# A fused attention and gated feed-forward kernel: batch 0 loaded by hardware queues in fp32, GpSimd's loads gated, a new order on eight PSUM banks

## The chip, the cores and the metric

The kernel runs on one core of a Trainium2 chip. The metric is device time in microseconds (us) of one execution. It is longer than the span of the profile (first to last instruction).

A ratio in this document is the mean time of one kernel's fast runs over that of the other's fast runs of the same rounds. So it is not quite the ratio of the medians that are quoted beside it. "Before" ran beside everything: its median was 224.40 us in the first rounds and 225.06, 224.94, 224.89 and 225.20 us in the later ones. For that reason results of different rounds are compared by their ratios to before.

## The reference

```python
B, H, S, Ns, D = 8, 8, 512, 32, 64            # x: (B,H,S,D), state: (B,H,Ns,D), fp32
scores = x @ state^T / sqrt(D);  a  = softmax(scores);   xread = a  @ state     # 512 rows
scores2 = state @ x^T / sqrt(D); a2 = softmax(scores2);  sread = a2 @ x         #  32 rows
rows = concat([xread, sread])                 # per batch 544 rows of H*D = 512
out  = (relu(rows @ w_gate) * (rows @ w_val)) @ w_out      # d_ff = 1536, fp32 out
```

## The kernel before

The kernel folds the attention's second product into the feed-forward part. Per batch it makes U = state times a weight column block ("c" and "u" units). It then multiplies U by the transposed attention weights ("gv": four matmuls of 512 columns), applies relu on ScalarE and the product on VectorE, and multiplies by w_out ("o"). It has two parts. The first, for batches 0, 1 and some of 2, is an explicit list of steps; here it is called the ordered part. Its matmuls write into eight PSUM buffers, called banks, which are handed from step to step. The rest is a loop that the change doesn't touch.

```python
def x_T(b, j):                    # transposes of one pair of heads
    ...
    for c in range(NC):
        if b == 0 and j < 2:      # heads 0-3 of batch 0: cast on chip, 128x128 transposes
            nc.tensor.transpose(ps[:, c], x_head(b)[:, c, 2*j:2*j+2]..., id128)
        else:                     # cast on load: head-major layout, two 64-wide transposes
            for h2 in range(2):
                nc.tensor.transpose(ps[64*h2:64*h2+64, c], v[:, c, h + h2], id128)
...
def bank(name, kind="r"):         # the ordered part names its PSUM bank ("@3");
    if given: n = given.pop(0)    # the loop behind takes 0,1,2,... in turn
    ...
    else: n = turn["r"] % 6 if kind == "r" else 6 + turn["o"] % 2
...
for eng, j in ((nc.sync, 0), (nc.scalar, None), (nc.scalar, 1)):   # fp32, hardware queues
    ...                           # None: state of batches 0 and 1
make_identity(nc, id128)
...
xb_alloc(0)                       # heads 4-7 of batch 0, cast to bf16 by GpSimd's DMA
nc.gpsimd.dma_start(out=x_tail(0)..., in_=x[0, HK:H]...)
...
program = """                     # dx: batch load, dw: weight columns, xc: cast, spin: warm-up
dx.1.0.2 dx.1.1.2 stc.0.0.act stc.0.1.dve spin.7 stT.0@0 xc.0.0.dve dw.0.0.128 sto.0.act dw.1.0.128 on xc.0.1.dve
spin.3 xT.0.1@1 dw.0.128.128 xT.0.0@2 ... sc.0.0@3 ... xT.0.2@4 xT.0.3@5 ... sc.0.1@0 ...
... gv.2.0@21 mu.1.8 re.2.0 o.0.7 mu.2.0 o.0.8 o.0.9@7 of.0.2.dve sr.1@3 sn.1 xp.2 xp.3
"""
```

The softmax here doesn't subtract the row's maximum and nothing guards it: scores larger than these inputs give would overflow.

Of the kernel before, what the change touches and what calls it, by code (L numbers as in the profile page):

```python
# [16 lines left out]
def kernel(  # L17
# [37 lines left out]
    NK = 2  # L55
# [18 lines left out]
    tiny = const.tile([128, 1], FP32, name="tiny")  # L74

# [68 lines left out]
    def x_conv_pair(b, j, eng):  # L144
        dst = x_head(b)[:, :, 2 * j:2 * j + 2].rearrange("p c h d -> p h c d")
        copy[eng](out=dst, in_=xf[b][:, 2 * j:2 * j + 2])

    def x_head(b):
        return xb[b][:, 0:NC * HK * D].rearrange("p (c h d) -> p c h d", c=NC, h=HK)

    def x_tail(b):
        return xb[b][:, NC * HK * D:].rearrange("p (h c d) -> p c h d", c=NC, h=HK)
# [9 lines left out]
    def x_T(b, j):  # L162

        if b not in xT:
            xT_alloc(b)
        ps = bank("xT_ps").bitcast(BF16)[:, 0:512].rearrange("p (c t) -> p c t", c=NC)
        for c in range(NC):
            if b == 0 and j < 2:
                nc.tensor.transpose(ps[:, c], x_head(b)[:, c, 2 * j:2 * j + 2].rearrange("p h d -> p (h d)"), id128)
            else:  # L170
                v, h = (x_tail(b), 2 * j - HK) if b == 0 else (xb[b], 2 * j)
                for h2 in range(2):
                    nc.tensor.transpose(ps[64 * h2:64 * h2 + 64, c], v[:, c, h + h2], id128)
        held["xT", b, j] = ps
# [63 lines left out]
    def att_T2(b):  # L238
        ans_alloc(b)
        ps = held["aT2", b] = bank("aT_ps").bitcast(BF16).rearrange("p (k c t) -> p k c t", k=NK, c=NC)  # L240
        for kc in range(NK):
            for c in range(NC):
                nc.tensor.transpose(ps[:, kc, c], a_sn[b][:, kc, c], id128)

    def att_out2(b, eng):
        copy[eng](out=ANS[b], in_=held["aT2", b])

# [3 lines left out]
    def x_pad(b):  # L251

        v = xa[:, b % NX].rearrange("p (c h) d -> p h c d", c=NC)[:, :, :, 0:D]
        for hs, src in (((0, x_head(b)), (HK, x_tail(b))) if b == 0 else ((0, xb[b]),)):
            src = src.rearrange("p c h d -> p h c d")
            nc.gpsimd.tensor_copy(out=v[:, hs:hs + src.shape[1]], in_=src)  # L256
# [153 lines left out]

    xb_alloc(0)
    nc.gpsimd.dma_start(out=x_tail(0).rearrange("p c h d -> p h c d"),  # L412
                        in_=x[0, HK:H].rearrange("h (p c) d -> p h c d", c=NC))

    def x_load(b, part, parts):
        if part == 0:
            xb_alloc(b)
            xb[b] = xb[b].rearrange("p (h c d) -> p c h d", h=H, c=NC)
# [11 lines left out]
    def spin(n, cols=512):  # L430
        for i in range(n):
# [4 lines left out]
    steps = {"spin": spin, "stc": state_conv, "stT": state_T, "sto": state_out, "xc": x_conv_pair, "xT": x_T, "xT2": x_T2, "xo2": x_out2, "on": lambda: nc.gpsimd.memset(xa[:, :, :, D:D + 1], 1.0), "dw": w_load, "dx": x_load, "ds": lambda: state_dma(nc.gpsimd, 2, B), "do": wo_dma,  # L436
             "df": lambda b: x_dma(b, (nc.gpsimd,)), "xo": x_out,
             "sc": att_sc, "ex": att_exp, "nr": att_sum, "nx": att_scale, "aT2": att_T2, "ao2": att_out2, "aT": att_T, "ao": att_out,
# [3 lines left out]
    dx.1.0.2 dx.1.1.2 stc.0.0.act stc.0.1.dve spin.7 stT.0@0 xc.0.0.dve dw.0.0.128 sto.0.act dw.1.0.128 on xc.0.1.dve  # L442
    spin.3 xT.0.1@1 dw.0.128.128 xT.0.0@2 xo.0.1.dve xo.0.0.act dw.1.128.128 spin.3 sc.0.0@3 dw.0.256.256 ex.0.0
    spin.1 xT.0.2@4 xT.0.3@5 xo.0.2.dve dw.1.256.256 xo.0.3.act nr.0.0 spin.3 sc.0.1@0 dw.0.512.256 xT2.1.0@1 ex.0.1
    nx.0.0 xo2.1.0.act nr.0.1 dw.1.512.256 spin.2 xT2.1.1@2 xo2.1.1.act sc.1.0@3 dw.0.768.256 nx.0.1 ex.1.0
    dw.1.768.256 spin.2 c.1.0.128@45 c.0.0.128@01 co.1.0.128.0.dve aT.0.1@2 co.0.0.128.0.act aT.0.0@3 co.1.0.128.1.dve
    co.0.0.128.1.act dw.0.1024.256 sc.1.1@4 ao.0.1.dve ao.0.0.act nr.1.0 ex.1.1 dw.1.1024.256 spin.2 c.0.128.128@05
    gv.0.0@12 co.0.128.128.1.act nr.1.1 co.0.128.128.0.act nx.1.0.pool re.0.0 gv.0.1@34 mu.0.0 re.0.1 nx.1.1.pool
    c.1.128.128@50 mu.0.1 co.1.128.128.1.act c.0.256.256@12 co.1.128.128.0.act c.1.256.256@30 dw.0.1280.256
    co.0.256.256.0.dve co.0.256.256.1.act aT.1.1@5 aT.1.0@4 co.1.256.256.0.act co.1.256.256.1.dve dw.1.1280.256  # L450
    gv.0.3@21 ao.1.1.act ao.1.0.dve dx.2.0.1 re.0.3 gv.0.2@30 mu.0.3 ds re.0.2 c.1.512.256@54 mu.0.2 gv.1.2@21
    co.1.512.256.1.act co.1.512.256.0.act do.0.6 c.0.512.256@30 re.1.2 gv.1.5@45 co.0.512.256.0.dve xp.1
    co.0.512.256.1.act mu.1.2 re.1.5 gv.1.3@23 mu.1.5 re.1.3 gv.1.1@04 do.6.12 mu.1.3 re.1.1 c.1.768.256@15 xp.0
# [124 lines left out]
```

## Time and profile before

| before, first trace | |
|---|---|
| time | 224.46 us median of 3 runs (224.29 to 224.59) |
| span of the profiled execution | 223.9 us (its own time was 225.65 us) |
| TensorE busy | 96% |
| first weights of 128 columns landed | 11.6 and 12.3 us |
| first weight matmul, first gv | 12.38, 14.43 us |
| ordered part ends on TensorE | 57.28 us |

From the page of before come the span, the busy time of each engine with its share of the span, the DMA engines' busy share in 40 slices of 5.6 us (9 is 90% or more), and the chain of waits:

```profile
span 223.9 us, 4840 instructions
PE 215.5 (96%) x1937; PEld 105.8 (47%) x1967; DVE 129.0 (58%) x226; ACT 124.8 (56%) x236; POOL 53.0 (24%) x58
...
DMA  7999999070146671781159114511311111111132
...
PE 84%; DMA 9%; POOL 4%; issue 2%; DVE 0%; POOLq 0%; DVEq 0%
```

TensorE is the bottleneck, and the DMA engines are full from the second slice to the seventh (5.6 to 39 us). So only the start can move much: once data and weights are there, the matmuls are dense. Next the timeline of before (start, duration, engine, line, instruction). POOL is GpSimd; its DMA lines are the time in which it issues the load, not the transfer.

```profile
1.42 0.98 POOL L412 DMA_DIRECT2D xb<-in_x_dram  x1
2.40 1.50 POOL L420 DMA_DIRECT2D xb<-in_x_dram  x2
...
12.38 0.25 PE L291 MATMUL upc<-wg_sb,stT 64*32 64x128 bf16 x8
...
14.43 1.93 PE L316 MATMUL gv_ps<-ans,U 128*128 128x512 bf16 x8
```

GpSimd issues from 1.42 us on; the first weight matmul follows the landing of its weights (12.3) at once. The same start in windows of 1 us: for each engine its busy time, then the TensorE clock, the DMA share (1 or more means that the 16 engines are full) and the GB/s written:

```profile
4.00:5.00 1.00, 1.00 (x6) 0.56 (x6) 0.82 (x3) 0.30 (x2) 1.00 (x2) 1.00 1.30 241
5.00:6.00 1.00, 0.92 (x9) 0.42 (x8) 0.63 (x1) 0.56 (x1) 1.00 (x3) 1.00 1.28 165
6.00:7.00 1.00, 0.97 (x10) 0.36 (x8) 0.43 (x1) 0.58 (x1) 1.00 (x3) 1.00 1.35 179
```

The DMA share (last column but one) never falls below 1. A casting load reads twice what it writes, so 180 GB/s written is about 360 read.

### The profile page before, as it was taken

Reading aid. Unit: us, or ns where it says so; the run is one execution under the profiler, and the core shown is the slowest. Engines: PE = TensorE matmul, PEld = TensorE weight load, DVE = VectorE, ACT = ScalarE, POOL = GpSimd, SP = SyncE. Lnnn points to the kernel's source line nnn. Section 1 sums busy time; section 2 is a strip of 40 time slices with the busy share of each in tenths; the row PEclk is TensorE's granted clock in tenths of the full one; section 3 lists DMA queues with packets and bytes.
Section 4 is the critical chain, followed back from the end, with each engine's and each line's share of the span. In section 5 each row is a group of like instructions: output and inputs, shape, how many; then the busy total and the mean of one; then the engine's idle time right before and its main releaser. Section 6 shows DMA issues by size and latency. Waiting matters only on the chain.

```text
span 223.9 us, 4840 instructions
## 1 busy us (share of the span) xinstructions
PE 215.5 (96%) x1937; PEld 105.8 (47%) x1967; DVE 129.0 (58%) x226; ACT 124.8 (56%) x236; POOL 53.0 (24%) x58
## 2 busy tenths in 40 slices
PE   7899999999999999999999999999999999999994
PEld 2544354444544444444444444444444445666543
DVE  3587888757595648663876468646874433222100
ACT  4599877865467644665557456545655444222221
POOL 8698828503302434006000700000000000000000
PEclk9999999999999999999999999999999999999999
DMA  7999999070146671781159114511311111111132
GB/s 157 176 195 197 215 225 278 24 187 3 47 106 225 112 267 47 160 265 50 50 118 276 49 60 99 107 50 47 94 50 47 48 47 50 48 64 74 54 94 94
DMA packets 37799, 25.48 MB, mean 114 GB/s; under 512 B 18864, under 2 KB 33200, under 8 KB 37776
## 3 DMA queue, kind: packets, MB, share of 16 engines
q1 hardware_dynamic: 24912, 16.85, 26.2%
q0 software_dynamic: 11968, 7.47, 21.5%
q10 hardware_dynamic: 896, 0.85, 1.4%
q8 instruction: 15, 0.25, 0.4%
q14 instruction: 8, 0.07, 0.1%
HBM read 18.35 MB, written 8.91 MB: 122 GB/s over the span
## 4 chain that ended last, share of the span: by engine, by line
PE 84%; DMA 9%; POOL 4%; issue 2%; DVE 0%; POOLq 0%; DVEq 0%
PE o_ps L353 38%; PE gv_ps L316 31%; DMA xb<-in_x_dram 9%; PE gv_ps L333 5%; PE up L291 4%; PE sr_ps L264 1%; POOL wv_sb L110 1%; PE sc_ps L200 1%; PE o_ps L379 1%; POOL wg_sb L110 1%; POOL a_sn L219 1%; PE xT_ps L186 0%; POOL xb L412 0%; PE stT_ps L129 0%; POOL xb L420 0%
## 5 line engine op out<-in xcount | busy, mean ns | idle before, releaser
L316 PE MATMUL gv_ps<-ans,U 128*128 128x512 bf16 x373 | 93.9, 380 | 0.5
L353 PE MATMUL o_ps<-wo_sb,h_sb 128*128 128x512 bf16 x357 | 91.6, 380 | 2.1 <-issue 1.9
L344 DVE TENSOR_TENSOR h_sb<-gv_ps,g_sb 128x512 bf16<-128x512 f32 x96 | 65.3, 689 | 44.2 <-ACT g_sb L340 43.3
L340 ACT ACTIVATE g_sb<-gv_ps 128x512 bf16<-128x512 f32 (+1 forms) x108 | 62.7, 580 | 49.3 <-PE gv_ps L316 34.5
L316 PEld LDWEIGHTS <-U 128*128 128x128 bf16 x384 | 35.8, 98 | 40.5 <-issue 0.6
L353 PEld LDWEIGHTS <-h_sb 128*128 128x128 bf16 x372 | 35.2, 98 | 39.9 <-issue 1.7
L361 ACT COPY o_sb<-o_ps 128x512 f32<-128x512 f32 x29 | 17.1, 590 | 16.5 <-PE o_ps L353 16.5
L301 ACT CAST U<-up 128x512 bf16<-128x512 f32 x36 | 18.9, 594 | 11.4 <-PE up L291 11.4
L301 DVE CAST U<-up 128x512 bf16<-128x512 f32 x36 | 22.8, 684 | 2.2 <-PE up L291 1.9
L142 POOL CAST xb<-xf 128x1024 bf16<-128x1024 f32 x10 | 10.1, 1040 | 53.6 <-DMA xf<-in_x_dram 32.6
L256 POOL COPY xa<-xb 128x2048 bf16<-128x2048 bf16 (+1 forms) x9 | 15.7, 1747 | 11.5 <-issue 6.6
L213 DVE TENSOR_REDUCE cs<-e_sn 128x16 f32<-128x512 bf16 x16 | 10.9, 683 | 7.7 <-ACT e_sn L207 7.7
L344 DVE TENSOR_TENSOR hs_sb<-gv_ps,g_sb 128x256 bf16<-128x256 f32 x12 | 5.1, 425 | 15.3 <-PE gv_ps L333 10.5
L207 ACT ACTIVATE e_sn<-sc_ps 128x512 bf16<-128x512 f32 x16 | 9.6, 600 | 5.6 <-PE sc_ps L200 5.5
L291 PEld LDWEIGHTS <-stT 64*32 64x32 bf16 x512 | 5.7, 90 | 11.2 <-issue 10.0
L311 ACT CAST U<-upc 128x512 bf16<-128x512 f32 (+1 forms) x20 | 9.6, 532 | 1.4 <-PE upc L291 1.3
L219 DVE TENSOR_TENSOR a_sn<-e_sn,rc 128x512 bf16<-128x512 bf16 x12 | 8.5, 709 | 0.6
L432 PE MATMUL warm_ps<-hs_sb 128*128 128x512 bf16 x20 | 7.2, 470 | 1.4 <-DVE hs_sb L396 1.2
L200 PEld LDWEIGHTS <-xT 128*128 128x128 bf16 x128 | 5.7, 98 | 3.8 <-ACT xT L177 0.7
L291 PE MATMUL up<-wg_sb,stT 64*32 64x512 bf16 x144 | 7.4, 383 | 0.0
L333 PE MATMUL gv_ps<-br,wg_sb 128*128 128x256 bf16 x48 | 7.2, 273 | 0.1
L333 PE MATMUL gv_ps<-br,wv_sb 128*128 128x256 bf16 x48 | 7.2, 273 | 0.0
(64 smaller groups left out, 129.5 us busy)
## 6 DMA issues: line engine op xcount, KB each, us to landing
out_dram<-o_sb SPq DMA_DIRECT2D x31, 256.0 KB, 2.3
xf<-in_x_dram SPq DMA_DIRECT2D x4, 1024.0 KB, 6.0
wo_sb<-in_moe_w_out_dram POOLq DMA_DIRECT2D x2, 768.0 KB, 15.4
wg_sb<-in_moe_w_gate_dram POOLq DMA_DIRECT2D x5, 256.0 KB, 8.7
wv_sb<-in_moe_w_val_dram POOLq DMA_DIRECT2D x5, 256.0 KB, 10.5
xf<-in_x_dram POOLq DMA_DIRECT2D x1, 1024.0 KB, 16.0
xb<-in_x_dram POOLq DMA_DIRECT2D x3, 256.0 KB, 7.1
xb<-in_x_dram POOLq DMA_DIRECT2D x1, 512.0 KB, 12.5
```

Source lines behind the costliest of these rows:

```text
L142: copy[eng](out=xb[b][:, :, hs].rearrange("p c h d -> p h c d"), in_=xf[b][:, hs])
L213: nc.vector.reduce_sum(out=cs, in_=e_v, axis=AX.X)
L219: {"dve": nc.vector, "pool": nc.gpsimd}[eng].tensor_tensor(out=by_pair(a_sn[b], jp).rearrange("p r (j n) -> p r j n", n=Ns), in0=e_v, in1= ...
L256: nc.gpsimd.tensor_copy(out=v[:, hs:hs + src.shape[1]], in_=src)
L291: nc.tensor.matmul(dst[parity][32 * j:32 * j + 32], stT[r:r + 64, b, j, 32 * parity:32 * parity + 32], wsb[r:r + 64, j, lo:lo + n], start= ...
L301: copy[eng](out=U[b][:, w, kc, lo:lo + 512], in_=held["u", b, w, lo][kc])
L316: nc.tensor.matmul(ps[w], U[b][:, w, kc, f0:f0 + 128], ANS[b][:, kc].rearrange("p c t -> p (c t)"), start=(kc == 0), stop=(kc == NK - 1))
L333: nc.tensor.matmul(ps[w][:, 0:nt], wsb[:, j, f0:f0 + 128], br[:, j].rearrange("p b n -> p (b n)"), start=(j == 0), stop=(j == NJ - 1))
L340: nc.scalar.activation(out=g_sb[:, 0:n], in_=ps[0][:, 0:n], func=AF.Relu)
L344: nc.vector.tensor_tensor(out=dst, in0=ps[1][:, 0:n], in1=held["g", b, jf][:, 0:n], op=ALU.mult)
L353: nc.tensor.matmul(held["o", b, tsub], src[:, jf, tsub * 128:(tsub + 1) * 128], wo_sb[:, jf], start=(jf == 0), stop=(jf == NF - 1))
L361: copy[eng](out=o_sb, in_=held["o", b, tsub])
```

## The change

The intent: bring all of batch 0 in by the two hardware queues, whose transfers come sooner (in the trace of before they landed at 3.7 to 4.9 us, GpSimd's first load at 8.2), and keep GpSimd's traffic away until the first heads have landed. All of batch 0 is then cast on chip, in the layout that needs half the transposes. The list of steps is computed anew, on all eight PSUM banks instead of six plus two.

```diff
+    gate = const.tile([128, 1], FP32, name="gate")
 ...
-    for eng, j in ((nc.sync, 0), (nc.scalar, None), (nc.scalar, 1)):
+    for eng, j in ((nc.sync, 0), (nc.scalar, None), (nc.sync, 2), (nc.scalar, 1), (nc.scalar, 3)):
 ...
     make_identity(nc, id128)
+    nc.gpsimd.memset(xa[:, :, :, D:D + 1], 1.0)
+    nc.gpsimd.tensor_copy(out=gate, in_=xf[0][:, 0, 0, 0:1])     # waits for heads 0 and 1
 ...
-    xb_alloc(0)
-    nc.gpsimd.dma_start(out=x_tail(0).rearrange("p c h d -> p h c d"),
-                        in_=x[0, HK:H].rearrange("h (p c) d -> p h c d", c=NC))
 ...      (x_T: batch 0 always by 128x128 transposes; x_pad: one copy for batch 0)
     program = """
-    dx.1.0.2 dx.1.1.2 stc.0.0.act stc.0.1.dve spin.7 stT.0@0 xc.0.0.dve dw.0.0.128 sto.0.act dw.1.0.128 on xc.0.1.dve
+    stc.0.0.dve stc.0.1.act xc.0.0.act dx.1.0.2 spin.7 xT.0.0@0 dx.1.1.2 xc.0.1.dve stT.0@1 xo.0.0.act xT.0.1@2
+    xc.0.2.dve dw.0.0.128 sto.0.dve xo.0.1.act dw.1.0.128 xc.0.3.act spin.1 sc.0.0@3 dw.0.128.128 xT.0.3@4 ex.0.0
 ...      (all steps reordered; four scalings go from GpSimd to VectorE; 15 warm-up matmuls instead of 23)
-    gv.2.0@21 mu.1.8 re.2.0 o.0.7 mu.2.0 o.0.8 o.0.9@7 of.0.2.dve sr.1@3 sn.1 xp.2 xp.3
+    o.0.9@6 mu.2.0 sr.1@2 sr.0@1 sn.1 sn.0 xp.2 xp.3
```

More of the change, by code (lines that the diff above doesn't have):

```diff
@@ L107, in xb_alloc @@
         xb[b] = att.tile([128, NC * H * D], BF16, name="xb", tag="xb", bufs=4)
+    cast_on_load = set()
     def w_dma(src, dst, lo, hi):
@@ L144, in x_conv_pair @@
     def x_conv_pair(b, j, eng):
-        dst = x_head(b)[:, :, 2 * j:2 * j + 2].rearrange("p c h d -> p h c d")
-        copy[eng](out=dst, in_=xf[b][:, 2 * j:2 * j + 2])
-    def x_head(b):
-        return xb[b][:, 0:NC * HK * D].rearrange("p (c h d) -> p c h d", c=NC, h=HK)
-    def x_tail(b):
-        return xb[b][:, NC * HK * D:].rearrange("p (h c d) -> p c h d", c=NC, h=HK)
+        if b not in xb:
+            xb_alloc(b)
+            xb[b] = xb[b].rearrange("p (c h d) -> p c h d", c=NC, h=H)
+        conv_heads(b, slice(2 * j, 2 * j + 2), eng)
     def xT_alloc(b):
@@ L167, in x_T @@
         for c in range(NC):
-            if b == 0 and j < 2:
-                nc.tensor.transpose(ps[:, c], x_head(b)[:, c, 2 * j:2 * j + 2].rearrange("p h d -> p (h d)"), id128)
-            else:
-                v, h = (x_tail(b), 2 * j - HK) if b == 0 else (xb[b], 2 * j)
-                for h2 in range(2):
-                    nc.tensor.transpose(ps[64 * h2:64 * h2 + 64, c], v[:, c, h + h2], id128)
+            if b in cast_on_load:
+                for h2 in range(2):
+                    nc.tensor.transpose(ps[64 * h2:64 * h2 + 64, c], xb[b][:, c, 2 * j + h2], id128)
+            else:
+                nc.tensor.transpose(ps[:, c], xb[b][:, c, 2 * j:2 * j + 2].rearrange("p h d -> p (h d)"), id128)
         held["xT", b, j] = ps
@@ L236, in att_T @@
         held["aT", b, kc] = ps
-    def att_T2(b):
-        ans_alloc(b)
-        ps = held["aT2", b] = bank("aT_ps").bitcast(BF16).rearrange("p (k c t) -> p k c t", k=NK, c=NC)
-        for kc in range(NK):
-            for c in range(NC):
-                nc.tensor.transpose(ps[:, kc, c], a_sn[b][:, kc, c], id128)
-    def att_out2(b, eng):
-        copy[eng](out=ANS[b], in_=held["aT2", b])
     def att_out(b, kc, eng):
@@ L251, in x_pad @@
     def x_pad(b):
-        v = xa[:, b % NX].rearrange("p (c h) d -> p h c d", c=NC)[:, :, :, 0:D]
-        for hs, src in (((0, x_head(b)), (HK, x_tail(b))) if b == 0 else ((0, xb[b]),)):
-            src = src.rearrange("p c h d -> p h c d")
-            nc.gpsimd.tensor_copy(out=v[:, hs:hs + src.shape[1]], in_=src)
+        v = xa[:, b % NX].rearrange("p (c h) d -> p c h d", c=NC)[:, :, :, 0:D]
+        nc.gpsimd.tensor_copy(out=v.rearrange("p c h d -> p h c d"), in_=xb[b].rearrange("p c h d -> p h c d"))
     def sr_mm(b, kind="r"):
@@ L409, in w_load @@
         w_dma((moe_w_gate, moe_w_val)[w], (wg_sb, wv_sb)[w], lo, lo + n)
-    xb_alloc(0)
-    nc.gpsimd.dma_start(out=x_tail(0).rearrange("p c h d -> p h c d"),
-                        in_=x[0, HK:H].rearrange("h (p c) d -> p h c d", c=NC))
     def x_load(b, part, parts):
         if part == 0:
+            cast_on_load.add(b)
             xb_alloc(b)
@@ L432, in spin @@
             nc.tensor.matmul(warm_ps[:, 0:cols], warm[:, 0:128], warm[:, 0:cols], start=True, stop=True)
-    steps = {"spin": spin, "stc": state_conv, "stT": state_T, "sto": state_out, "xc": x_conv_pair, "xT": x_T, "xT2": x_T2, "xo2": x_out2, "on": lambda: nc.gpsimd.memset(xa[:, :, :, D:D + 1], 1.0), "dw": w_load, "dx": x_load, "ds": lambda: state_dma(nc.gpsimd, 2, B), "do": wo_dma,
+    steps = {"spin": spin, "stc": state_conv, "stT": state_T, "sto": state_out, "xc": x_conv_pair, "xT": x_T, "xT2": x_T2, "xo2": x_out2, "dw": w_load, "dx": x_load, "ds": lambda: state_dma(nc.gpsimd, 2, B), "do": wo_dma,
              "df": lambda b: x_dma(b, (nc.gpsimd,)), "xo": x_out,
-             "sc": att_sc, "ex": att_exp, "nr": att_sum, "nx": att_scale, "aT2": att_T2, "ao2": att_out2, "aT": att_T, "ao": att_out,
+             "sc": att_sc, "ex": att_exp, "nr": att_sum, "nx": att_scale, "aT": att_T, "ao": att_out,
              "c": c_unit, "co": c_out, "u": u_unit, "uo": u_out, "gv": gv, "re": relu, "mu": mult, "o": out_part,
@@ L441 @@
     program = """
-    dx.1.0.2 dx.1.1.2 stc.0.0.act stc.0.1.dve spin.7 stT.0@0 xc.0.0.dve dw.0.0.128 sto.0.act dw.1.0.128 on xc.0.1.dve
-    spin.3 xT.0.1@1 dw.0.128.128 xT.0.0@2 xo.0.1.dve xo.0.0.act dw.1.128.128 spin.3 sc.0.0@3 dw.0.256.256 ex.0.0
-    spin.1 xT.0.2@4 xT.0.3@5 xo.0.2.dve dw.1.256.256 xo.0.3.act nr.0.0 spin.3 sc.0.1@0 dw.0.512.256 xT2.1.0@1 ex.0.1
-    nx.0.0 xo2.1.0.act nr.0.1 dw.1.512.256 spin.2 xT2.1.1@2 xo2.1.1.act sc.1.0@3 dw.0.768.256 nx.0.1 ex.1.0
-    dw.1.768.256 spin.2 c.1.0.128@45 c.0.0.128@01 co.1.0.128.0.dve aT.0.1@2 co.0.0.128.0.act aT.0.0@3 co.1.0.128.1.dve
@@ L447 @@
-    co.0.0.128.1.act dw.0.1024.256 sc.1.1@4 ao.0.1.dve ao.0.0.act nr.1.0 ex.1.1 dw.1.1024.256 spin.2 c.0.128.128@05
-    gv.0.0@12 co.0.128.128.1.act nr.1.1 co.0.128.128.0.act nx.1.0.pool re.0.0 gv.0.1@34 mu.0.0 re.0.1 nx.1.1.pool
-    c.1.128.128@50 mu.0.1 co.1.128.128.1.act c.0.256.256@12 co.1.128.128.0.act c.1.256.256@30 dw.0.1280.256
-    co.0.256.256.0.dve co.0.256.256.1.act aT.1.1@5 aT.1.0@4 co.1.256.256.0.act co.1.256.256.1.dve dw.1.1280.256
-    gv.0.3@21 ao.1.1.act ao.1.0.dve dx.2.0.1 re.0.3 gv.0.2@30 mu.0.3 ds re.0.2 c.1.512.256@54 mu.0.2 gv.1.2@21
@@ L452 @@
-    co.1.512.256.1.act co.1.512.256.0.act do.0.6 c.0.512.256@30 re.1.2 gv.1.5@45 co.0.512.256.0.dve xp.1
-    co.0.512.256.1.act mu.1.2 re.1.5 gv.1.3@23 mu.1.5 re.1.3 gv.1.1@04 do.6.12 mu.1.3 re.1.1 c.1.768.256@15 xp.0
-    mu.1.1 gv.1.4@23 co.1.768.256.0.act co.1.768.256.1.act c.0.768.256@04 re.1.4 gv.1.0@15 co.0.768.256.0.dve
-    co.0.768.256.1.act df.3 mu.1.4 re.1.0 gv.1.6@20 mu.1.0 re.1.6 gv.0.4@41 mu.1.6 re.0.4 gv.0.6@35 mu.0.4 re.0.6
-    gv.1.7@20 mu.0.6 re.1.7 c.0.1024.256@41 c.0.1280.256@35 mu.1.7 co.0.1024.256.0.act xT2.2.0@2 stc.1.0.pool
@@ L457 @@
-    co.0.1024.256.1.act co.0.1280.256.1.dve xT2.2.1@0 stc.1.1.pool co.0.1280.256.0.act xo2.2.0.dve gv.0.5@41
-    stc.3.0.pool stc.3.1.pool xo2.2.1.dve re.0.5 stc.2.1.pool gv.0.10@53 stc.2.0.pool mu.0.5 re.0.10 stT.1@2 gv.0.9@40
-    mu.0.10 sto.1.act re.0.9 sc.2.1@1 gv.0.8@52 ex.2.1 mu.0.9 re.0.8 nr.2.1 gv.0.11@34 re.0.11 mu.0.8 gv.0.7@10
-    nx.2.1.pool mu.0.11 re.0.7 sc.2.0@5 o.0.0@6 mu.0.7 ex.2.0 nr.2.0 c.1.1280.256@32 c.1.1024.256@14
-    co.1.1280.256.1.act u.2.1.1024@50 o.0.1 co.1.1024.256.0.dve co.1.1024.256.1.act nx.2.0.pool uo.2.1.1024.1.dve
@@ L462 @@
-    uo.2.1.1024.0.act o.0.2 co.1.1280.256.0.act u.2.0.0@21 xn.3 of.0.0.dve u.2.1.0@45 uo.2.0.0.1.act u.2.1.512@03
-    uo.2.1.0.0.dve o.0.3@7 uo.2.1.0.1.act uo.2.0.0.0.dve uo.2.1.512.0.act aT.2.0@1 aT.2.1@4 uo.2.1.512.1.dve
-    ao.2.0.act o.0.4 ao.2.1.act o.0.5 gv.2.1@50 of.0.1.act re.2.1 gv.1.10@23 mu.2.1 re.1.10 gv.1.11@14 mu.1.10 re.1.11
-    gv.2.3@50 mu.1.11 re.2.3 gv.2.2@23 mu.2.3 re.2.2 u.2.0.1024@14 u.2.0.512@50 mu.2.2 uo.2.0.1024.1.act sr.0@2
-    o.0.6@6 uo.2.0.512.1.act uo.2.0.512.0.dve sn.0 gv.1.9@34 uo.2.0.1024.0.dve re.1.9 gv.1.8@05 mu.1.9 re.1.8
@@ L467 @@
-    gv.2.0@21 mu.1.8 re.2.0 o.0.7 mu.2.0 o.0.8 o.0.9@7 of.0.2.dve sr.1@3 sn.1 xp.2 xp.3
+    stc.0.0.dve stc.0.1.act xc.0.0.act dx.1.0.2 spin.7 xT.0.0@0 dx.1.1.2 xc.0.1.dve stT.0@1 xo.0.0.act xT.0.1@2
+    xc.0.2.dve dw.0.0.128 sto.0.dve xo.0.1.act dw.1.0.128 xc.0.3.act spin.1 sc.0.0@3 dw.0.128.128 xT.0.3@4 ex.0.0
+    xT.0.2@5 xo.0.3.dve dw.1.128.128 xo.0.2.act nr.0.0 spin.3 sc.0.1@6 dw.0.256.256 xT2.1.0@0 ex.0.1 nx.0.0
+    dw.1.256.256 xo2.1.0.act nr.0.1 spin.2 xT2.1.1@1 dw.0.512.256 sc.1.0@2 xo2.1.1.dve dw.1.512.256 ex.1.0 nx.0.1
@@ new lines @@
+    spin.1 sc.1.1@3 dw.0.768.256 c.0.0.128@45 ex.1.1 nr.1.0 aT.0.0@6 aT.0.1@0 dw.1.768.256 co.0.0.128.1.act
+    c.1.0.128@12 co.0.0.128.0.act ao.0.0.dve ao.0.1.act dw.0.1024.256 nr.1.1 spin.1 c.0.128.128@35 co.1.0.128.1.act
+    gv.0.0@46 co.0.128.128.0.act dw.1.1024.256 nx.1.0 co.0.128.128.1.act re.0.0 gv.0.1@02 dw.0.1280.256 nx.1.1
+    co.1.0.128.0.act re.0.1 mu.0.0 aT.1.1@3 aT.1.0@5 dw.1.1280.256 ao.1.1.dve c.1.128.128@74 c.0.256.256@10 ao.1.0.dve
+    co.1.128.128.0.act c.1.256.256@63 co.0.256.256.0.dve co.0.256.256.1.act gv.1.0@57 co.1.256.256.1.act dx.2.0.1
@@ new lines @@
+    co.1.256.256.0.dve re.1.0 gv.0.3@01 mu.0.1 co.1.128.128.1.act re.0.3 mu.1.0 ds c.0.512.256@36 c.1.512.256@54
+    co.0.512.256.1.act co.0.512.256.0.dve gv.1.2@20 co.1.512.256.1.act co.1.512.256.0.dve do.0.6 re.1.2 gv.0.4@76
+    mu.0.3 xp.1 re.0.4 mu.1.2 gv.1.1@34 mu.0.4 re.1.1 gv.0.5@52 mu.1.1 re.0.5 do.6.12 c.0.768.256@17 c.1.768.256@03
+    mu.0.5 co.0.768.256.0.act gv.1.5@64 xp.0 co.1.768.256.0.act co.1.768.256.1.dve re.1.5 gv.0.2@52 co.0.768.256.1.dve
+    re.0.2 mu.1.5 gv.1.4@10 df.3 mu.0.2 re.1.4 gv.1.7@36 mu.1.4 re.1.7 c.1.1024.256@75 c.0.1280.256@42 mu.1.7
@@ new lines @@
+    co.1.1024.256.1.act gv.0.6@10 co.0.1280.256.0.act co.1.1024.256.0.dve re.0.6 gv.1.3@36 co.0.1280.256.1.dve re.1.3
+    mu.0.6 gv.1.9@54 mu.1.3 re.1.9 c.1.1280.256@71 stc.1.0.pool c.0.1024.256@23 mu.1.9 stc.1.1.pool
+    co.1.1280.256.1.act gv.0.11@06 stc.2.1.pool co.0.1024.256.0.act co.0.1024.256.1.dve stc.3.0.pool re.0.11
+    gv.0.10@54 co.1.1280.256.0.dve stc.3.1.pool stc.2.0.pool re.0.10 mu.0.11 gv.0.9@12 mu.0.10 re.0.9 gv.0.7@30 mu.0.9
+    re.0.7 stT.1@7 gv.1.11@56 mu.0.7 sto.1.act re.1.11 u.2.0.0@41 u.2.1.1024@23 mu.1.11 uo.2.0.0.0.act u.2.1.0@70
@@ new lines @@
+    xT2.2.0@5 uo.2.1.1024.0.act uo.2.1.0.1.dve xT2.2.1@4 uo.2.1.1024.1.act xo2.2.0.dve gv.0.8@62 uo.2.1.0.0.act
+    xo2.2.1.dve uo.2.0.0.1.act gv.1.10@03 re.0.8 re.1.10 o.0.0@7 mu.0.8 mu.1.10 gv.1.6@54 re.1.6 xn.3 sc.2.1@1 o.0.1
+    mu.1.6 ex.2.1 nr.2.1 u.2.0.512@02 u.2.0.1024@35 uo.2.0.512.0.act u.2.1.512@14 o.0.2 uo.2.0.512.1.dve
+    uo.2.1.512.0.act nx.2.1 uo.2.0.1024.1.act o.0.3@6 of.0.0.act uo.2.1.512.1.act sc.2.0@0 o.0.4 uo.2.0.1024.0.act
+    ex.2.0 o.0.5 nr.2.0 gv.1.8@21 of.0.1.act nx.2.0 re.1.8 o.0.6@7 mu.1.8 aT.2.1@5 o.0.7 ao.2.1.dve aT.2.0@4 o.0.8
@@ L468 @@
+    ao.2.0.act gv.2.2@30 of.0.2.act re.2.2 gv.2.3@21 mu.2.2 re.2.3 gv.2.1@54 mu.2.3 re.2.1 gv.2.0@30 mu.2.1 re.2.0
+    o.0.9@6 mu.2.0 sr.1@2 sr.0@1 sn.1 sn.0 xp.2 xp.3
     """
```

## The prediction

> **What bounds the kernel now.** TensorE is busy 96% of 223.9 us (busy table); the chain of waits is 84% TensorE. The ordered part (to the second sr matmuls) ends at 57.3 us in the timeline; the rest, which the change leaves alone, is 166.6 us of dense matmuls. From 14.4 us (first gate/value matmuls, "gv") to 57.3 I count 40.1 us of needed TensorE work at traced rates (28 gv units and 10 output parts of 0.864, the rest small), so only 2.7 us of losses. The start is what can move, and two things bind it. (1) DMA: by windows, the engines are full from 2.6 to 39.5 us, at 360 to 400 GB/s read, and weights land just when used: the first pair at 11.6 and 12.3, first weight matmul at 12.38; value columns 256 to 511 at 16.8, used at 16.86. (2) From 10 to 20 us ScalarE is busy 9.4 of 10, VectorE 8.7.
>
> **What changes.** Heads 4 to 7 of batch 0 (512 KB) move from a casting GpSimd load (issued 1.42, landed 8.2) to hardware queues; they should land at 5.5 to 6.2. They cost two casts (0.65 us each) on ScalarE/VectorE, and save 8 transposes. Four scales of a_sn go from GpSimd (1.04) to VectorE (0.69). Batch 0's second scores should come at about 8.8 instead of 9.47.
>
> But GpSimd's queue starts later. Its first issue waits for heads 0 and 1 (landed 4.2): about 4.4 instead of 1.42. In the trace its first packet moved at 4.2, 2.8 us after the issue began (the Trainium skill, "DMA: Bandwidth & Descriptors", Specifications, gives about 1 us; this trace shows more). So its data starts at 6.0 to 7.1, while the hardware queues, 1.15 MB at 385 packets of 1 KB per us, run dry at about 5.65. The same page (Issuing engines are not separate DMA queues) says that all run on the same 16 engines; the trace agrees (the software queue filled as the hardware ones drained), so moving bytes between queues gains no bandwidth and a gap is lost. Against before, ahead by 390 packets at 6.9 us, I estimate every GpSimd load 1.1 us later (0.4 to 1.5): batch 1's halves at 10.6 and 11.9 (before 9.5, 10.8), first weights at 12.7 and 13.4.
>
> **Critical path.** With those landings and traced durations, summed along each engine's new order: first weight matmul 13.6, first gv 15.2 (14.43), fourth gv ends 20.8 with both 256-column units done (19.8). Lag 1.0 us; later uses are far enough behind their loads that TensorE is dense. Pairing the U units and eight banks save perhaps 0.3 us. Net +0.5: the order may have been computed for landings that I misjudge, which could make it 0.5 to 1 us faster.
>
> **Prediction: 225.0 us, 80% range 223.3 to 226.7. Faster by over 2%: 0.01; within 2%: 0.96; slower by over 2%: 0.03.**
>
> **What would show it.** DMA share well below full between about 5.6 and 6.9 us; first batch 1 half landing after 10 us, first weights after 12.7; first weight matmul after 13; ordered part ending at 57.3 to 58.5; the time behind it 166.6. Wrong, if GpSimd's data follows the gate within 1.3 us, weights land by 12.3, or the first gv starts before 14.4.
>
> **What would make it wrong.** The 2.8 us of start-up may be partly a first-use cost; then the change gains up to 1.5 us. ScalarE carries a long run of copies from 13.5 to 20 us; a slip there costs TensorE directly. Eight fewer warm-up matmuls leave gaps near 4.4 and 9.3 us; if the clock (the first seven took 0.43 us each, later ones 0.22) wakes later, a few tenths more.

## The result and the profile after

The changed kernel took 225.19 us (median of 4, 224.93 to 225.30) against 224.40 us for before (4 runs). The ratio is 1.0033, 95% interval 1.0015 to 1.0050: a third of a per cent slower.

The page of the changed kernel:

```profile
span 223.4 us, 4803 instructions
PE 213.7 (96%) x1922; PEld 105.9 (47%) x1951; DVE 130.4 (58%) x229; ACT 125.2 (56%) x239; POOL 48.4 (22%) x53
...
DMA  6999999271065682681169113501311111111132
...
PE 89%; DMA 5%; POOL 2%; issue 1%; DVE 1%; ACT 0%; DVEq 0%
```

This span, 223.4, is *shorter* than that of before, 223.9, though the kernel is slower. The two traces alone would give the wrong sign. The changed kernel's span fits its timed runs (225.16 us for that execution, against a median of 225.19). The trace of before is the odd one of its rounds, and its own time says so (225.65 against 224.40). Experiment 1 settles it. The timeline of the changed kernel, the start and the end of the ordered part:

```profile
4.09 0.19 POOL L392 COPY gate<-xf 128x1 f32<-128x1 f32 x1 [2.48 <-DMA xf<-in_x_dram]
4.22 1.71 POOL L405 DMA_DIRECT2D xb<-in_x_dram  x2
...
11.95 0.25 PE L277 MATMUL upc<-wg_sb,stT 64*32 64x128 bf16 x8
...
13.56 1.90 PE L302 MATMUL gv_ps<-ans,U 128*128 128x512 bf16 x8
...
55.20 0.70 PE L250 MATMUL sr_ps<-xa,e_sn 128*32 128x65 bf16 x64
55.84 0.39 PE L302 MATMUL gv_ps<-ans,U 128*128 128x512 bf16 x1
56.66 0.60 PE L302 MATMUL gv_ps<-ans,U 128*128 128x512 bf16 x2 [0.43 <-DVE sn L259]
```

Two things are new. GpSimd waits for the first heads until 4.09 and issues at 4.22. And behind the ordered part, the first gv stops before its third matmul (the second's record is missing from the trace) and waits 0.43 us for VectorE's `sn`. About 0.22 us of this idle time is the unrecorded matmul: in the traces of experiments 7 and 9, which kept all four records of this gv, the wait shown is 0.21. The windows of 1 us of the changed kernel:

```profile
4.00:5.00 1.00, 0.61 (x4) 0.27 (x4) 0.00 (x0) 0.68 (x2) 0.91 (x2) 1.00 1.09 376
5.00:6.00 1.00, 1.00 (x12) 0.86 (x10) 0.84 (x2) 0.59 (x1) 1.00 (x3) 1.00 0.54 167
6.00:7.00 1.00, 0.82 (x8) 0.27 (x6) 0.50 (x2) 0.71 (x2) 1.00 (x2) 1.00 0.81 95
```

Here is the hole that the prediction named: the hardware queues drain at about 5.5 us (376 GB/s in fp32 in the microsecond before, share 0.54 in the sixth). GpSimd's first packets come at 5.87, 1.65 us behind the issue, and the bulk at about 6.2, 2.0 us behind it. In before, GpSimd's queue took over without a gap.

### The profile page after: what moved, and what is told of

Its sections match the earlier page's. It is cut to its first block, busy times and chain, and to the rows that moved or that the text cites. A ratio compares the mean times of both kernels' runs of the same rounds, so it can differ in the third digit from the quotient of the medians.

```text
span 223.4 us, 4803 instructions
## 1 busy us (share of the span) xinstructions
PE 213.7 (96%) x1922; PEld 105.9 (47%) x1951; DVE 130.4 (58%) x229; ACT 125.2 (56%) x239; POOL 48.4 (22%) x53
## 4 chain that ended last, share of the span: by engine, by line
PE 89%; DMA 5%; POOL 2%; issue 1%; DVE 1%; ACT 0%; DVEq 0%
PE o_ps L339 38%; PE gv_ps L302 36%; PE gv_ps L319 5%; PE up L277 4%; DMA wv_sb<-in_moe_w_val_dram 3%; DMA xf<-in_x_dram 1%; PE sc_ps L198 1%; PE o_ps L365 1%; PE sr_ps L250 1%; PE upc L277 1%; POOL wg_sb L113 1%; POOL xb L405 1%; POOL wv_sb L113 1%; PE xT_ps L184 0%; DVE h_sb L330 0%
## 5 line engine op out<-in xcount | busy, mean ns | idle before, releaser
L347 ACT COPY o_sb<-o_ps 128x512 f32<-128x512 f32 x31 | 18.3, 590 | 16.7 <-PE o_ps L339 16.7
L287 ACT CAST U<-up 128x512 bf16<-128x512 f32 x40 | 20.9, 597 | 11.4 <-PE up L277 11.3
L145 POOL CAST xb<-xf 128x1024 bf16<-128x1024 f32 x10 | 10.6, 1086 | 56.5 <-DMA xf<-in_x_dram 44.9
L287 DVE CAST U<-up 128x512 bf16<-128x512 f32 x32 | 20.2, 682 | 2.2 <-PE up L277 1.9
L242 POOL COPY xa<-xb 128x2048 bf16<-128x2048 bf16 x8 | 15.2, 1901 | 12.3 <-issue 12.1
L217 DVE TENSOR_TENSOR a_sn<-e_sn,rc 128x512 bf16<-128x512 bf16 x16 | 12.3, 771 | 0.4
L277 PEld LDWEIGHTS <-stT 64*32 64x32 bf16 x512 | 5.7, 90 | 10.3 <-issue 8.4
L297 ACT CAST U<-upc 128x512 bf16<-128x512 f32 (+1 forms) x18 | 8.2, 508 | 1.9 <-PE upc L277 1.9
L277 PE MATMUL up<-wv_sb,stT 64*32 64x512 bf16 x144 | 7.1, 379 | 0.0
```

Source lines behind the costliest of these rows:

```text
L145: copy[eng](out=xb[b][:, :, hs].rearrange("p c h d -> p h c d"), in_=xf[b][:, hs])
L217: {"dve": nc.vector, "pool": nc.gpsimd}[eng].tensor_tensor(out=by_pair(a_sn[b], jp).rearrange("p r (j n) -> p r j n", n=Ns), in0=e_v, in1= ...
L242: nc.gpsimd.tensor_copy(out=v.rearrange("p c h d -> p h c d"), in_=xb[b].rearrange("p c h d -> p h c d"))
L277: nc.tensor.matmul(dst[parity][32 * j:32 * j + 32], stT[r:r + 64, b, j, 32 * parity:32 * parity + 32], wsb[r:r + 64, j, lo:lo + n], start= ...
L287: copy[eng](out=U[b][:, w, kc, lo:lo + 512], in_=held["u", b, w, lo][kc])
L347: copy[eng](out=o_sb, in_=held["o", b, tsub])
```

## Experiments

All ran five rounds.

### 1. The kernel before once more

No edit.

> The kernel before, unchanged, timed and profiled once more. Its first profile came from an execution of 225.65 us, while its unprofiled executions took 224.3 to 224.6, so that trace may be of an unusually slow execution. Theory A (the slow-sample theory): the new profile has a span of 222.4 to 222.9 us, with the first weights landing before 11.2 us instead of 11.6 and 12.3, and the first gate/value matmuls before 14.0 us instead of 14.43. Theory B (the first profile is typical and the two kernels differ outside the span): span 223.7 to 224.1 again, first gate/value matmuls at 14.4.

Measured: 225.11 us (224.83 to 225.67) beside 225.06 for the same kernel's other runs, ratio 1.0011, interval 0.9994 to 1.0028. This null comparison shows what the method resolves: differences of 0.1% mean nothing. Span 223.1 us. The timeline of this second trace of before:

```profile
11.77 0.25 PE L291 MATMUL upc<-wg_sb,stT 64*32 64x128 bf16 x8
...
13.82 1.92 PE L316 MATMUL gv_ps<-ans,U 128*128 128x512 bf16 x8
...
56.16 0.43 PE L264 MATMUL sr_ps<-xa,e_sn 128*32 128x65 bf16 x32
56.53 1.04 PE L316 MATMUL gv_ps<-ans,U 128*128 128x512 bf16 x3
57.40 1.03 PE L353 MATMUL o_ps<-wo_sb,h_sb 128*128 128x512 bf16 x4
58.26 0.40 PE L200 MATMUL sc_ps<-stT,xT 128*128 128x64 bf16 x8
```

The first weights landed at 10.8 and 11.5 instead of 11.6 and 12.3, and everything on TensorE is 0.6 to 0.8 us earlier. Theory A holds in substance, though the span came out 0.2 us above its range: the first trace was of a slow start. (Such starts aren't rare: in the later rounds before itself took up to 225.78 and 226.28 us in single runs.) From batch 3's first scores (58.26 here, 59.02 in the first trace) to the last output's issue, the two traces agree within 0.01 us at the start of every group of scores. So of the 0.8 us between these two executions, 0.6 arise before the first gv, where the loads land, and nearly all of the rest before batch 3's first scores.

### 2. The changed kernel once more

No edit.

> The changed kernel, unchanged, once more: 1.002 to 1.005 of before, span 223.2 to 223.6, first gate/value matmuls at 13.4 to 13.7. Theory A and B agree here; it fixes the size of the difference, in the same rounds as the other three.

Measured: 225.51 us (225.09 to 225.65), ratio 1.0020 (1.0004 to 1.0036), span 223.8. First gv at 14.54, a full microsecond later than in the first trace of the changed kernel and outside what I had expected; the first weights landed at 11.8 and 12.6 (10.8 and 11.5 in its first trace). One line of its timeline shows what came last:

```profile
11.17 0.64 PE L184 MATMUL xT_ps<-id,xb 128*64 128x128 bf16 x16 [1.25 <-DMA xb<-in_x_dram]
```

TensorE waits 1.25 us for the second half of batch 1, which landed at 11.13 (10.05 in the first trace). So the changed kernel scatters as well, and one pair of traces must not be read as the difference. With the traces of 1 and 2, whose executions ran in the same rounds, the difference can be laid out:

| stretch | before | changed | difference |
|---|---|---|---|
| start to first gv | 13.82 | 14.54 | +0.72 |
| first gv to batch 3's first scores | 44.45 | 44.16 | -0.28 |
| these scores to the last output's issue | 161.99 | 161.93 | -0.06 |
| last output's issue to the end | 2.83 | 3.17 | +0.34 |
| span | 223.1 | 223.8 | +0.72 |

The middle -0.28 contains the wait on `sn` and is thus better than it looks; the first +0.72 contains the loads. The clock has no part in it here: in this trace of the changed kernel TensorE ran at full rate from 4.64 us on (128x128 transposes of 0.22 us, 0.31 where it is at half rate). The other experiments take the rows one by one.

### 3. No gate

```diff
-    nc.gpsimd.tensor_copy(out=gate, in_=xf[0][:, 0, 0, 0:1])
```

> The changed kernel without the gate: GpSimd's first load is issued at about 1.6 us instead of 4.22, and its packets share the DMA engines with batch 0's. Theory of the prediction (the hole in the DMA stream behind the gate delays every weight): hole at 5.5 to 6.2 us gone, weights land 0.6 to 1.2 us earlier, time 0.3 to 1.0 us shorter than the changed kernel. Rival (the weights are not what TensorE waits for, or batch 0's heads come later by as much as the weights gain): within 0.2 us of the changed kernel, or slower, with heads 4 to 7 landing after 6.5 us instead of 5.1 to 6.0.

Measured: 226.40 us median. The five fast runs took from 224.15 to 227.41; a sixth, of 227.87, counts as slow (over 1.5% above the fastest) and is left out of the ratio, 1.0042 (1.0001 to 1.0082). The hole is gone and the first weights landed at 11.1 and 11.9, 0.7 earlier than in 2, as the prediction's theory said; yet heads 6 and 7 landed at 7.6 instead of 6.1, as the rival said, and batch 0's second scores came at 10.43 instead of 8.41. GpSimd's first packet moved only at 5.37, 3.9 us behind its issue at 1.46, when the hardware queues had almost drained; in the second trace of before, issued at 1.43 with 0.52 MB less on the hardware queues, it moved at 3.78. In this trace TensorE was idle from 7.2 to 8.3 us, and its granted clock was 0.50 from 7.89 to 11.30 us. That the one caused the other isn't shown. These are its windows of 1 us (the clock is the last column but two):

```profile
7.00:8.00 1.00, 0.20 (x7) 0.07 (x3) 0.00 (x0) 0.35 (x1) 0.62 (x1) 0.94 1.25 155
8.00:9.00 1.00, 0.68 (x7) 0.69 (x8) 0.04 (x1) 0.76 (x2) 0.00 (x0) 0.50 1.50 175
9.00:10.00 1.00, 1.00 (x7) 0.45 (x4) 0.98 (x2) 0.59 (x1) 0.75 (x1) 0.50 1.72 182
```

So the gate isn't useless. In this trace GpSimd's packets ran beside those of batch 0's last heads from 5.4 us on, and these landed 1.5 us later. The gate trades that against a hole. The median can't be compared finely, given the spread.

### 4. The gate on an earlier load

```diff
-    nc.gpsimd.tensor_copy(out=gate, in_=xf[0][:, 0, 0, 0:1])
+    nc.gpsimd.tensor_copy(out=gate, in_=st_f[:, 0, 0, 0:1])
```

> The changed kernel with the gate moved to the state load, which lands about 0.5 us before heads 0 and 1, so GpSimd's first load is issued at about 3.6 us instead of 4.22 and its first packet comes at about 5.5 instead of 6.2, just as the hardware queues drain. Theory of the prediction: hole closed, weights 0.5 to 0.7 us earlier, time 0.2 to 0.6 us shorter than the changed kernel. Rival: no change within 0.2 us.

Measured: 224.89 us (224.06 to 225.28), ratio 0.9992 (0.9973 to 1.0012), so 0.28% or 0.6 us better than the changed kernel in the same rounds (1.0020), though the intervals overlap a little. GpSimd issued at 3.49 instead of 4.11. The gain is as large as the shift of 0.62 us, at the top of the expected range. The single trace doesn't show it well: first weights at 11.4 and 12.2, 0.4 earlier than in 2, but first gv at 14.72. In that execution warm-up matmuls still took 0.43 us each at 8.3 us, and the first weight matmul came 0.9 us behind its weights, so something else came last there.

### 5. The gate on a later load

This doubles the suspected cost.

```diff
-    nc.gpsimd.tensor_copy(out=gate, in_=xf[0][:, 0, 0, 0:1])
+    nc.gpsimd.tensor_copy(out=gate, in_=xf[0][:, 2, 0, 0:1])
```

> The changed kernel with the gate on heads 4 and 5 instead of heads 0 and 1 (the second issue of the same queue, which lands about 1.2 us later), so GpSimd's first load is issued at about 5.2 us instead of 4.2: the suspected cost about doubled. Theory (a later start of GpSimd's queue delays every weight one for one, and TensorE waits for them): the hole in the DMA share is 1.0 us longer, first weights land 0.8 to 1.2 us later than with the gate as changed, 0.6 to 1.1 us longer than the changed kernel, so 1.005 to 1.008 of before. Rival (the hole is free, since the start is bound by ScalarE's and VectorE's chains): 1.002 to 1.004.

Measured: 226.90 us (226.32 to 227.05), ratio 1.0091 (1.0074 to 1.0107). That is 0.6 to 0.7 percentage points above the changed kernel's two results, 1.3 to 1.6 us. The edit doesn't do quite what the expectation says: index 2 of `xf[0]` is head 2, so the gate waited for heads 2 and 3, the second load of ScalarE's queue (landed at 5.18), and not for heads 4 and 5 (landed at 6.25, behind GpSimd's issue). GpSimd issued at 5.61, 1.4 to 1.5 us later than with the gate as changed, since the gate's copy began at 5.23 and took 0.44 us instead of 0.19. So the dose was larger than planned, and so was the answer. Its windows of 1 us:

```profile
5.00:6.00 1.00, 1.00 (x12) 0.80 (x10) 0.43 (x1) 0.59 (x1) 0.77 (x2) 1.00 0.52 176
6.00:7.00 1.00, 0.72 (x4) 0.24 (x3) 0.73 (x2) 0.67 (x2) 1.00 (x2) 1.00 0.00 0
7.00:8.00 1.00, 0.83 (x13) 0.83 (x13) 0.11 (x1) 0.65 (x2) 1.00 (x2) 1.00 0.51 58
```

The DMA engines stand still for the whole seventh microsecond, the first weights land at 12.8 and 13.6, and first gv comes at 15.46. Together with 4: over a range of 2.1 us of GpSimd's issue time, the kernel's time follows it about one for one. That the start of GpSimd's queue is on the critical path in this range is shown, not only argued. (Below it, with the issue at 1.46, experiment 3 gained nothing.)

### 6. Old order, new loads

The changed kernel's loads, casts and gate with the old list of steps; only the two new casts are added to it.

```diff
-    ... sto.0.act dw.1.0.128 on xc.0.1.dve
-    spin.3 xT.0.1@1 dw.0.128.128 xT.0.0@2 xo.0.1.dve xo.0.0.act dw.1.128.128 spin.3 sc.0.0@3 ...
+    ... sto.0.act dw.1.0.128 xc.0.1.dve
+    spin.3 xT.0.1@1 dw.0.128.128 xT.0.0@2 xc.0.2.act xo.0.1.dve xo.0.0.act xc.0.3.dve dw.1.128.128 spin.3 sc.0.0@3 ...
```

> The new loads, casts and gate with the order and six banks of the kernel before (the two further casts put in front of the first scores). Theory (loads cost, order gains): first gv 0.5 to 1.0 us later than in the kernel before (13.8 in its second trace), the part from there to the end of the ordered part as before (44.4 to 44.6 us to the first scores of batch 3), 1.002 to 1.005 of before. Rival (the loads are free and the order loses): 0.998 to 1.001.

Measured: 225.89 us (225.55 to 226.25), ratio 1.0042 (1.0028 to 1.0055): +0.95 us. First gv at 14.56, 0.74 later than in the second trace of before. From there to batch 3's scores it took 44.99 us, 0.4 more than expected. By itself, the new way of loading costs about a microsecond in the old order.

### 7. New order, old loads

The kernel before with the new list of steps on eight banks, less the two casts.

```diff
-    dx.1.0.2 dx.1.1.2 stc.0.0.act stc.0.1.dve spin.7 stT.0@0 ...      (old list)
+    stc.0.0.dve stc.0.1.act xc.0.0.act dx.1.0.2 spin.7 xT.0.0@0 dx.1.1.2 xc.0.1.dve stT.0@1 xo.0.0.act xT.0.1@2
+    dw.0.0.128 sto.0.dve xo.0.1.act dw.1.0.128 on spin.1 sc.0.0@3 ...     (new list, xc.0.2 and xc.0.3 left out)
```

> The order and eight banks of the changed kernel with the loads of the kernel before (GpSimd at once, heads 4 to 7 of batch 0 cast on load). Theory (loads cost, order gains): the part from the first gv to batch 3's scores takes 43.8 to 44.2 us instead of 44.4 to 44.6, although it holds the 0.65 us bank wait; first gv within 0.4 us of 13.8; 0.997 to 1.000 of before. Rival (the order loses): 1.001 to 1.004.

Measured: 224.64 us (223.41 to 225.13), ratio 0.9981 (0.9958 to 1.0004): -0.4 us, with an interval that touches 1. First gv at 13.99, and 43.71 us from there to batch 3's scores, still better than expected. So the order gains about half of what the loads lose: 0.9981 for the order alone, 1.0042 for the loads alone and 1.0020 to 1.0033 for both, so the two about add up.

### 8. Another bank for the state-read matmuls

```diff
-    o.0.9@6 mu.2.0 sr.1@2 sr.0@1 sn.1 sn.0 xp.2 xp.3
+    o.0.9@6 mu.2.0 sr.1@2 sr.0@5 sn.1 sn.0 xp.2 xp.3
```

The loop behind the ordered part takes banks 0, 1, 2 in turn. In the changed kernel bank 1 still holds batch 0's state read (`sr.0@1`), which VectorE reads last of all (`sn.0`); before had used banks 2 and 3.

> The changed kernel with one bank number changed: batch 0's state-read matmuls at the end of the ordered part take bank 5 instead of bank 1, which the untouched rest of the kernel asks for at once. In both traces of the changed kernel TensorE's first gv behind the ordered part waits 0.43 us there for VectorE to read that bank (0.65 us with the pipeline restart). Theory (that wait is real loss): 0.5 to 0.7 us shorter than the changed kernel, so 0.999 to 1.001 of before, and the gap between the last sr matmuls and the next scores of batch 3 falls from about 2.8 us to 2.1. Rival (the wait only stands in for another one): unchanged, 1.002 to 1.004.

Measured: 224.83 us (224.27 to 225.17), ratio 0.9990 (0.9975 to 1.0005). Its timeline:

```profile
55.65 0.71 PE L250 MATMUL sr_ps<-xa,e_sn 128*32 128x65 bf16 x64
56.29 1.04 PE L302 MATMUL gv_ps<-ans,U 128*128 128x512 bf16 x4
57.17 1.03 PE L339 MATMUL o_ps<-wo_sb,h_sb 128*128 128x512 bf16 x4
58.03 0.40 PE L198 MATMUL sc_ps<-stT,xT 128*128 128x64 bf16 x8
```

The wait is gone: 2.38 us from the sr matmuls to the next scores, against 2.76 in the first trace of the changed kernel. I had expected 2.1, since I had taken the gap of the missing record for a restart of the pipeline; the wait is worth 0.38 us, not 0.65. The timed gain against the changed kernel (0.3 to 0.4 percentage points, 0.7 to 1.0 us, across different rounds) is more than that; the rest is within the scatter of the starts. In this trace the granted clock was 0.50 from 7.28 to 10.69 us, as in experiment 3's, and first gv came only at 14.80. The direction is shown, the size only roughly.

### 9. The warm-up matmuls put back

```diff
-    spin.7 xT.0.0@0 ... stT.0@1 xo.0.0.act ... spin.1 sc.0.0@3 ... xT.0.3@4 ... spin.2 xT2.1.1@1 ... spin.1 sc.1.1@3
+    spin.8 xT.0.0@0 ... stT.0@1 spin.1.256 xo.0.0.act ... spin.2 sc.0.0@3 ... spin.1 xT.0.3@4 ... spin.4 xT2.1.1@1 ... spin.2 sc.1.1@3
```

> The changed kernel with the warm-up matmuls put back into the gaps of the first 12 us (one more at 4.2, half a one at 5.3, one each before the first scores, before the third transposes and before the last scores, two before batch 1's second transposes). Theory of the clock (fewer warm-ups let the clock wake late or go back to half in some executions, as the trace of the kernel without the gate shows at 8 to 11 us): all matmuls behind 5 us at full rate (0.22 us for 512 columns), 0.1 to 0.4 us shorter than the changed kernel. Rival (what TensorE waits for there are loads and copies, so its own rate does not matter): within 0.15 us of it, 1.002 to 1.004 of before.

Measured: 225.09 us (224.95 to 225.37), ratio 1.0007 (0.9995 to 1.0020). In its trace every matmul behind 5.2 us runs at full rate. The ratio lies below both results of the changed kernel (1.0020 and 1.0033), but the intervals overlap: a gain of 0.1 to 0.3% is likely and not proven. Its runs lie within 0.4 us; those of the changed kernel lay within 0.4 and 0.6, so no narrower spread is shown. The Trainium skill ("TensorE: Matmul & The Clock Gate", Part 1, on the clock gate) says that the activity window runs free of the kernel, so the moment of waking varies from run to run. The traces agree: the first four transposes took 0.61 us in the first trace of the changed kernel (cold) and 0.40 in its second (awake), from the same program. The other traces bear on the theory too. Of the seven with the new loads, the new order and 15 warm-ups, two (experiments 4 and 5) reached full rate only at 10.4 and 10.3 us and two (3 and 8) lost it again for 3.4 us from 7.9 and 7.3. None of the other seven traces (old order, old loads, or warm-ups refilled) had half rate behind 6.9 us. (The clock column shows 1.00 during the first cold stretch; there the matmuls' own times tell.)

### 10. The parts that gain, without the part that costs

Experiment 7 with the bank of experiment 8.

```diff
-    ... sr.1@2 sr.0@1 sn.1 sn.0 xp.2 xp.3
+    ... sr.1@2 sr.0@5 sn.1 sn.0 xp.2 xp.3
```

> New order and eight banks, the loads of the kernel before, and bank 5 for batch 0's state-read matmuls: the two parts that gained, without the part that cost. If the terms add (new order with old loads 0.998 of before, bank 0.6 us): 0.994 to 0.997 of before, and no wait of TensorE on VectorE behind the last sr matmuls. Rival (terms overlap, TensorE then waits for something else at the same place): 0.998 or more.

Measured: 223.60 us (223.25 to 224.38), ratio 0.9951 (0.9932 to 0.9970), span 221.6. It beats both kernels, by half a per cent over before. In its trace no wait follows the sr matmuls, the first weights landed at 10.3 and 11.0, and first gv came at 13.18. That is 0.8 us earlier than in experiment 7's trace, with the same loads, so part of its 0.7 us over experiment 7 may be the scatter of the starts; the bank's wait is 0.38 us.

### 11. The new loads made as good as I could

The changed kernel with the edits of 4, 8 and 9, and one more warm-up matmul.

> The changed kernel's loads made as good as I can: gate on the state load, bank 5, warm-ups refilled (3920 TensorE rows in the program, 247 ScalarE rows). If the terms add: 0.995 to 0.999 of before. It also tells which instruction stream makes the last 0.3 us of the changed kernel, a single instruction fetch behind the last output: if TensorE's (3904 to 3918 rows had it, 3920 and 3936 not), it is gone here and the time from the last output's issue to the end is 2.85 us; if ScalarE's (247 rows had it, 244 to 246 not), it stays and that time is 3.15 us.

Measured: 224.70 us (224.41 to 224.75), ratio 0.9989 (0.9975 to 1.0004). The terms of 4, 8 and 9 don't add up to what 10 gets from simply loading as before. In its trace GpSimd issued at 3.44 and the first weights landed at 10.8 and 11.6, but the first weight matmul came only at 12.76, behind batch 1's last scores (12.42) in TensorE's order: with the loads this early, the weights no longer came last. And the last 0.3 us stayed, which rules out the number of TensorE's instructions as I had supposed it.

### 12. One instruction fewer on ScalarE

```diff
-    ... of.0.2.act ... sr.1@2 sr.0@1 ...
+    ... of.0.2.dve ... sr.1@2 sr.0@5 ...
```

> The changed kernel with bank 5 (0.999 of before) and one output copy of the ordered part moved from ScalarE to VectorE, so that ScalarE's program has 246 rows instead of 247. Theory (the last 0.3 us is an instruction fetch that ScalarE's stream needs because it just crosses the end of a block): no instruction packet behind the last output, 2.85 us from the last output's issue to the end instead of 3.15, 0.997 to 0.999 of before. Rival (the fetch belongs to another stream, or to the loads): instruction packet and 3.15 us stay, 0.998 to 1.000.

Measured: 225.52 us (224.90 to 226.00) beside 225.20, ratio 1.0001 (0.9976 to 1.0026), and the packet and 3.17 us to the end are still there. My theory of ScalarE's stream fell. What the traces show of this term: these are the DMA queues (packets, MB, share of the engines) from 219 to 224.5 us in the second trace of before,

```profile
q1 hardware_dynamic: 233, 0.22, 11.1%
q10 hardware_dynamic: 288, 0.20, 10.9%
```

and in that of the changed kernel:

```profile
q1 hardware_dynamic: 288, 0.33, 16.6%
q10 hardware_dynamic: 288, 0.20, 11.1%
q14 instruction: 1, 0.01, 0.4%
```

All nine traces of programs with both the new loads and the new order fetch one instruction packet behind the last output and take 3.12 to 3.22 us from its issue to the end. The two of before and those of experiments 6, 7 and 10 don't fetch, and take 2.76 to 2.86. The Trainium skill ("Runtime: NRT & Kernel Launch", Instruction fetch mechanics) says that engines refill their instruction memory in blocks of 256 instructions and that a crossing is mostly hidden; if this packet is such a crossing, it is not hidden at the very end. That the packet costs the 0.3 us is inferred from the two going together in every trace; whose stream it is stays open.

## Why the prediction was right, and where it was not

The number was right: 225.0 predicted, 225.19 measured, and the sign (slightly slower). The mechanism was right in part: the time does follow the start of GpSimd's queue, but the hole alone doesn't make the loads late. Several terms were mis-sized and three were missing (a second dip of the DMA rate, the bank's wait, the end), so part of the agreement is luck, errors that cancelled.

- **Moving bytes to other queues gains no bandwidth, and a hole is lost.** Right that the hole comes, only in part about what it costs. The Trainium skill ("DMA: Bandwidth & Descriptors", Issuing engines are not separate DMA queues) says that all queues run on the same 16 engines, and the traces agree: one queue follows the other there. But the rates differ: 376 GB/s by the hardware queues (4 to 5 us), against 272 to 358 read by GpSimd's in the two traces of before (136 to 179 written, 5 to 7 us). The hole lies at 5.5 to 6.2 us; I had put it at 5.6 to 6.9. Experiments 4 and 5 show that GpSimd's issue time is paid about one for one, experiment 6 that the new loads cost 0.95 us in the old order. Yet counted at the source (what GpSimd writes counts double), the changed kernel's engines had moved 1.38 MB by 7.0 us against 1.58 in the first pair of traces, and 1.52 against 1.49 in the second: 0.2 MB behind or none, where I had reckoned 390 packets of 1 KB. In the second pair the loads fall behind only later, in a second dip of the rate (9 to 10 us; above the second trace of before, below that of the changed kernel; GB/s written last):

```profile
9.00:10.00 1.00, 1.00 (x26) 0.79 (x25) 0.93 (x3) 0.64 (x2) 0.75 (x1) 1.00 1.75 180
9.00:10.00 1.00, 0.76 (x15) 0.34 (x10) 1.00 (x2) 1.00 (x2) 1.00 (x2) 1.00 0.96 93
```

The prediction had no such dip. It goes with the loads and not with the order: from 9 to 10 us experiment 6's trace wrote 99 GB/s, experiment 7's 178. No run tells how the cost of the loads divides between it and the hole.
- **The delay between GpSimd's issue and its first packet, 2.8 us.** Mis-sized: 1.65 us behind the gate, 2.0 to the bulk. Experiment 3's trace points to the hardware queues' traffic as what lengthened it at the start: with 0.52 MB more on them the same issue time gave 3.9 us, against 2.35 and 2.75 in the two traces of before. No run was made to test this alone.
- **"I estimate every GpSimd load 1.1 us later (0.4 to 1.5)".** Wrong as a statement about every load. Against the second trace of before (8.7 and 10.0 for batch 1's halves, 10.8 and 11.5 for the first weights), the changed kernel's two traces had 8.6 and 10.0, 8.5 and 11.1 for the halves, and 10.8 and 11.5, 11.8 and 12.6 for the weights. Batch 1's first half is not late at all: with the hardware queues drained it landed 4.4 us after its issue, against 6.3 us in before. The first weights are 0 to 1.1 us late.
- **First weight matmul at 13.6, first gv at 15.2.** Too late: 11.95 and 12.94, 13.56 and 14.54. I had summed from the first trace of before, whose start was 0.6 us slower than that of the second. The first trace even trips my own test ("the first gv starts before 14.4"); the second doesn't. I should have seen that the traced execution was 1.1 us longer than every timed run of its rounds.
- **"Pairing the U units and eight banks save perhaps 0.3 us".** Mis-sized. With old loads the new order gains 0.4 us while it still holds the bank wait (the interval touches 1), and 1.1 us without it (experiments 7 and 10).
- **"The time behind it 166.6".** Wrong. It was 167.5 us (223.37 less 55.84). The parts are 0.38 us of wait for bank 1, at the seam between the ordered part and the loop, 0.3 us at the end, and a stall of 0.35 us at 88 us, whose cause I did not seek; one other of the nine traces has it too (0.27 us, experiment 3). I had costed the new order and its eight banks, but not who owns a bank when the untouched code asks for it. In the other traces the loop from batch 3's first scores on was 0.06 us shorter than in before.
- **The clock.** Named as a risk, and seen: the traces of experiments 3 and 8 had it at 0.50 for 3.4 us from 7.9 and 7.3 us, and those of 4 and 5 reached full rate only past 10 us. The refilled warm-ups of experiments 9 and 11 had full rate from 5.2 us at the latest; what that is worth in time isn't shown.

What stays open: the size of the clock term; whose instruction fetch ends the kernel; and why, in all but two of the traces with the new loads, the DMA rate dips a second time between batch 1's loads and the first weights (the lines above).

## What to carry to other kernels

When the DMA engines are already full, handing bytes to another queue brings little, and a gate in front of the next queue can leave the engines empty while it starts up (about 0.7 us here): compare when the first queue drains with when the next one's first packet can come. When an order is recomputed, check the seams, here a PSUM bank that the code behind asks for first; and test the order and the data movement apart, since here one gained about half of what the other lost. Before reading two traces against each other, compare each traced execution's own time with the timed runs; if one is off by more than the effect, trace it again.

## What the Trainium skill lacked or had wrong

- "DMA: Bandwidth & Descriptors", Specifications: about 1 us to the first byte of a GpSimd load. Here the first packet moved 2.35 to 2.8 us after the issue began in the traces with the old loads, 3.9 us after it with more loads on the hardware queues (experiment 3), and about 1.7 us after it behind the gate.
- The same page, on the anatomy of a GpSimd DMA, fits 2.0 us plus bytes over 436 GB/s. For batch 1's first half, which reads 0.52 MB, that gives an estimate of 3.2 us. Measured: 3.9 to 4.9 us in the traces with the gate on heads 0 and 1 or later, where the hardware queues drain first, and 6.3 us behind another GpSimd load in the second trace of before.
- None of the pages that I used speaks of the second dip of the DMA rate between loads with 1 KB and with 512-byte source rows (93 GB/s written for a microsecond, against some 160 before and after it).
- "Runtime: NRT & Kernel Launch", Instruction fetch mechanics, calls a block crossing mostly hidden; it doesn't say whether one at the end of a kernel shows. Here one packet, which may be such a fetch, goes with 0.3 us.
- "TensorE: Matmul & The Clock Gate" gives the free-running window, and the traces agree. How far it moves the moment of waking in a kernel whose start has gaps isn't given; here full rate began between 3.9 and 10.4 us in the seven traces with the new loads, the new order and 15 warm-ups.
